# A chunked attention with a bilinear feed-forward: weights of tiles 2 and 3 by halves of rows, values in PSUM tiles of their own, and the Out product of block 1 by Strassen

## The chip, the cores and the metric

The kernel runs on one core of a Trainium2 chip, as one launch. The metric is the device time of that launch in microseconds (us). Engines are named as in the profile: PE is TensorE, with PEld its loading of weights; DVE is VectorE; ACT is ScalarE; POOL is GpSimd; SP is SyncE, whose queue issues nearly all the transfers.

## What is computed

Attention within chunks of 64 tokens for 8 batches, 8 heads, 576 tokens and a head size of 64; then a bilinear feed-forward over all 4608 tokens, with a model size of 512 and an inner size of 1536.

```python
q_c, k_c, v_c = (t.reshape(B, H, nc, 64, D) for t in (q, k, v))
scores = scale * np.matmul(q_c, k_c.transpose(0, 1, 2, 4, 3))
scores = scores - np.max(scores, axis=-1, keepdims=True)
attn = np.exp(scores)
attn = attn / (np.sum(attn, axis=-1, keepdims=True) + 1e-09)
x = np.matmul(attn, v_c)          # then (B, H, S, D) -> (B * S, H * D)
a = x @ w_a
b = x @ w_b
out = (a * b) @ w_out
```

Inputs and output are fp32. The kernel multiplies in bf16 and accumulates in fp32.

## The kernel before

**Tiling.** The 4608 tokens are nine blocks K of 512. A block is made by two attention units of 256 tokens each, so there are 18 units; unit u belongs to block u // 2. In the feed-forward the inner size is 12 tiles (ft) of 128 and the model size four tiles of rows (kt). The weights are kept in bf16 in six pairs: wa[i] and wb[i] serve tiles 2i and 2i + 1.

**One block of the feed-forward.** `ffn(K, ft)` (L415) takes two PSUM banks. `ffn_products` (L393) makes b and a, four matmuls of 512 columns each; `ffn_close` (L407) lets ACT copy b to SBUF and DVE multiply it by a, which gives ab[ft]. The four banks F are handed out in turn by `nextF` (L108), so a bank comes free when its reader of two tiles ago is done. The normalised attention of a block is in xT[K % 3]; a matmul of 512 columns reads both of its units.

**The Out product** comes in two forms. The plain one (`outs`, L441, and `out_products`, L420) takes 12 matmuls of 512 columns for each of four groups of 128 tokens. `outs_fast(K, t)` (L471) does Strassen's scheme on 2 x 2 blocks: seven products of six matmuls with 256 columns, for two groups of tokens at once, called for t = 0 and t = 1. It needs sums of the weights (`wsum`, by `sum_wo`, L453: four instructions for each of six pairs) and of ab (`asum`, by `sum_ab`, L463: three DVE instructions per pair of tiles). In it ACT copies the products m3 and m4 out, POOL adds them (w, L525), DVE adds the third product p1 to w (L526), and DVE and POOL make the four outputs. Blocks 0 and 1 are done in the plain form, blocks 2 to 8 by Strassen. `wsum` lies over slots 2 to 5 of the weights' staging ring `wst`, and `asum` over slots 6 to 9, where w_out's pairs 0 to 3 are staged: a sum of ab can be written only when the sums of those pairs have been read from there.

**Order.** The whole program is under a manual schedule: each engine executes its instructions in the order in which the code issues them. The stages that the change touches:

- The prologue (L551 to L638) does units 0 and 1 from the first block's heads, in quarters. `half_values` (L368) makes the values of heads 4 to 7 in one call, `half_normalise` (L383) divides them by the sums into xT[0], and `fill` (L536) keeps PE at work on zeros. Tiles 0 and 1 of block 0 start on row tiles 0 and 1 (L640 to L653) and go on with rows 2 and 3. `queue_w` (L569) issues the loads of weights on SP's queue and `land_w` (L573) casts them on POOL: pair 0 by halves of the rows, pair 1 by halves of the columns, the others whole.
- Block 0's Out product (L757 to L779) is run together with unit 2's attention.
- Block 1's feed-forward (L792 to L829) is done in two halves of 256 tokens for tiles 0 to 9, then whole for tiles 10 and 11. Between these loops POOL casts units 5, 6 and 7 (`cast_unit`) and makes sums of w_out (`some_sums`), and SP's queue gets transposes (`turn_unit`) and loads of later units (`load_unit`).
- Block 1's Out product is L836 to L840, with `slot(5, None)` behind its first group. A `slot` (L690) makes sums and values of one unit and the scores of the next; its normalisations and exponentials are put on a list, and `step()` (L709) issues one of them, before each tile.

Of the kernel before, what the change touches and what calls it, by code (L numbers as in the profile page):

```python
# [11 lines left out]
def kernel(  # L12
# [10 lines left out]
    nc = tc.nc  # L23
# [74 lines left out]
    asum = asum.rearrange("p (i n t) -> p i n t", i=NP, n=5)  # L98
    part = buf("part", [128, 2, 5, HF], FP32)

    state = {"f": 0, "b": 0, "o": 0, "w": 2}

    def ring(name, bufs):
        i = state[name]
# [260 lines left out]
        s = slice(mm * 256, mm * 256 + 256)  # L365
        nc.scalar.activation(out=inv[hu][:, :, s], in_=lns[:, :, s], func=AF.Exp, scale=-1.0)

    def half_values(hu):  # L368
        for mm in range(2):
            for g in range(4):  # L370
                c = mm * 256 + g * 64
                for cl in range(2):
                    for j in range(2):
                        h = 2 * mm + j
                        nc.tensor.matmul(
                            PA[j * 64:j * 64 + 64, cl, c:c + 64],
                            vb[hu][cl * 64:cl * 64 + 64, g * 256 + h * 64:g * 256 + h * 64 + 64],
                            E[hu][cl * 64:cl * 64 + 64, j, c:c + 64],
                            start=True,
                            stop=True,  # L380
                        )

    def half_normalise(hu, mm):  # L383
        s = slice(mm * 256, mm * 256 + 256)
        nc.vector.tensor_tensor(  # L385
            out=xT[0][:, 2 * hu + mm, :].rearrange("p (g c t) -> p c g t", g=4, c=2),
            in0=PA[:, :, s].rearrange("p c (g t) -> p c g t", g=4),
            in1=inv[hu][:, :, s].rearrange("p c (g t) -> p c g t", g=4),
            op=MULT,
        )  # L390
# [69 lines left out]
            c0, c1, op = ((1, 3, SUB), (2, 0, SUB), (0, 3, ADD))[part - 1]  # L460
            eng.tensor_tensor(out=y[:, part + 1], in0=b[:, c0], in1=b[:, c1], op=op)

    def sum_ab(i):  # L463

        a = ab2[i].rearrange("p f (h t) -> p (f h) t", h=2)
        y = asum[:, i]
        nc.vector.tensor_tensor(out=y[:, 4], in0=a[:, 0], in1=a[:, 3], op=ADD)
        nc.vector.tensor_tensor(out=y[:, 0:2], in0=a[:, 0:2], in1=a[:, 2:4], op=ADD)  # L468
        nc.vector.tensor_tensor(out=y[:, 2:4], in0=a[:, 1:3], in1=a[:, 0:4:3], op=SUB)  # L469

    def outs_fast(K, t):  # L471
        c = t * 128
        m3, m4, w, y1, y2 = [part[:, t, n, :] for n in range(5)]
        oa, ob = ring("o", osb), ring("o", osb)
        V, A, G = nc.vector, nc.scalar, nc.gpsimd

        def product(a, b, o=None, pairs=range(NP)):
            o = nextF()[:, 0:HF] if o is None else o
            for i in pairs:
                nc.tensor.matmul(  # L480
                    o, a(i)[:, c:c + 128], b(i), start=(i == 0), stop=(i == NP - 1)
                )
            return o

        def of_ab(f, h):
            return lambda i: ab2[i][:, f, h * HF:(h + 1) * HF]

        def of_wo(f, h):
            return lambda i: wo[i][:, f, h * HF:(h + 1) * HF]

        def of_asum(n):
            return lambda i: asum[:, i, n]

        def of_wsum(n):
            return lambda i: wsum[:, i, n]

        def add(eng, out, in0, in1, op=ADD):
            eng.tensor_tensor(out=out, in0=in0, in1=in1, op=op)  # L498

        if K == NBLK - 1 and t == 1:  # L500

            A.copy(out=m3, in_=product(of_ab(0, 0), of_wsum(2)))
            A.copy(out=m4, in_=product(of_ab(1, 1), of_wsum(3)))
            add(G, w, m3, m4)
            add(V, oa[:, HF:DM], product(of_asum(0), of_wo(1, 1)), m3)
            add(G, y1, w, oa[:, HF:DM], SUB)
            add(V, ob[:, 0:HF], product(of_asum(1), of_wo(0, 0)), m4)
            add(G, y2, w, ob[:, 0:HF], SUB)
            p1 = product(of_asum(4), of_wsum(4))
            store(K, 2 + t, ob, 0, HF)  # L510
# [12 lines left out]
        product(of_asum(4), of_wsum(4), p1, (NP - 1,))  # L523
        A.copy(out=m4, in_=p4)  # L524
# [26 lines left out]
    with tc.manual_schedule():  # L551
# [21 lines left out]
        def land_w(i, halves=1, xs=(0,)):  # L573

            c = 256 // halves
            for x in xs:
                for h in range(halves):
                    for n, w in (("b", wb), ("a", wa)):
                        kts, st = staged[n, i][x]
                        copy(  # L580
                            G,
                            w[i][:, kts[0]:kts[-1] + 1, h * c:h * c + c],
                            st[:, :, h * c:h * c + c],
                        )

        def queue_wo(i):
            staged["o", i] = load_wo(i, nc.sync)
# [40 lines left out]
        quad_scores(3)  # L628
        expo(1, 1)
        half_inverse(0, 1)  # L630
        half_values(0)
        for mm in range(2):
            half_normalise(0, mm)
# [6 lines left out]
        B0 = [(nextF(), nextF()) for _ in range(2)]  # L640
        spare = PS[:, 0, :]
        for of in "ba":
            for kt in range(2):
                for ft in range(2):
                    ffn_products(0, ft, (0, 1), (kt,), B0[ft], of)
        half_values(1)
        for mm in range(2):
            half_normalise(1, mm)
        fill(3, spare, 256)
        for ft in range(2):  # L650
            for kt in range(2, NKT):
                ffn_products(0, ft, (0, 1), (kt,), B0[ft])
            ffn_close(0, ft, (0, 1), B0[ft])  # L653
        queue_w(3)


# [55 lines left out]
                fn(*a)  # L712

        for ft in range(1, NFT):
            if ft > 1:
                ffn(0, ft)
            if ft in (1, 2, 3, 4, 5):
                land_w(ft, 2 if ft == 1 else 1)
# [39 lines left out]
        for f0 in range(0, NFT, 2):  # L758

            for tgs in ((0, 1), (2, 3)):  # L760
# [139 lines left out]
```

## Time and profile before

| | us |
|---|---|
| median of 13 runs (313.19 to 315.03) | 314.36 |
| the profiled execution | 314.5 |
| its span, first to last instruction | 312.6 |
| PE busy in the span | 301.6 |
| DVE busy | 186.9 |
| ACT busy | 135.1 |
| POOL busy | 123.7 |

The span is 1.9 us shorter than the execution's time. The mean granted clock of TensorE is 0.999 of full speed. The table counts busy time alone; which wait ends last in a stage is read from the timelines.

Where the stages lie, by PE's timeline: the feed-forward of block 0 begins at 12.9 us, its Out product at 37.3, block 1 at 50.0, block 1's Out product at 74.8, block 2 at 85.9. Blocks 3 to 7 then take about 31.9 us each.

In a line of a timeline stand the start, the time from the start of the first to the end of the last instruction of the group, the engine, the line of the kernel, the operation, the tile written and the tiles read, shapes and the count; in brackets the idle time of the engine just before, and what ended it. "SPq" is SP's queue of DMA issues. A line of code can be that of a helper: L170 is every copy or cast, L498 every add of `outs_fast`.

### The profile page before, as it was taken

The page shows a single profiled execution, that of the slowest core. Times are in us where ns is not written, and L with a number is a line of the kernel's source. Part 1 is how long each engine was busy: PE and PEld are TensorE (multiplying, and loading weights), DVE is VectorE, ACT ScalarE, POOL GpSimd, SP SyncE. Part 2 cuts the span into 40 slices and gives each one's busy share as a digit, 9 for nine tenths or more (in the row PEclk, how much of TensorE's full clock was granted, in tenths as well). Part 3 has the DMA queues.
Part 4 walks back from the last instruction along what each step waited for, and adds up shares of the span by engine and source line. Part 5 has one row for each costly group of instructions (what it writes and reads, how often), then busy time and mean ns, then how long its engine had stood idle before and what let it go on. Part 6 is the DMA issues. An engine that isn't in the chain of part 4 may idle for free.

```text
span 312.6 us, 7316 instructions
## 1 busy us (share of the span) xinstructions
PE 301.6 (96%) x2897; PEld 178.9 (57%) x2930; DVE 186.9 (60%) x373; ACT 135.1 (43%) x232; POOL 123.7 (40%) x151
## 2 busy tenths in 40 slices
PE   6889999999999999999999999999999999999995
PEld 3444457884444486448644764476446744674474
DVE  3544325544369655866596649664967476746663
ACT  3822245655246533562355326532644164313220
POOL 2667757966576128302720273017401400040023
PEclk9999999999999999999999999999999999999999
DMA  7999999999999999989898339933600410020003
GB/s 261 294 348 388 380 307 221 215 248 222 238 214 288 209 235 231 234 187 205 236 251 186 73 143 230 237 68 136 136 0 2 96 41 1 2 112 25 0 1 136
DMA packets 144819, 55.01 MB, mean 176 GB/s; under 512 B 126224, under 2 KB 138768, under 8 KB 144784
## 3 DMA queue, kind: packets, MB, share of 16 engines
q1 hardware_dynamic: 143696, 53.49, 68.5%
q10 hardware_dynamic: 1088, 1.05, 1.0%
q8 instruction: 23, 0.38, 0.5%
q14 instruction: 12, 0.10, 0.1%
HBM read 37.75 MB, written 9.44 MB: 151 GB/s over the span
## 4 chain that ended last, share of the span: by engine, by line
PE 88%; DMA 5%; SPq 2%; issue 1%; POOL 1%; ACTq 0%; ACT 0%; DVE 0%; POOLq 0%; DVEq 0%
PE F L399 57%; PE F L480 20%; PE F L421 7%; DMA f<-in_k_dram 3%; DMA wst<-in_moe_w_a_dram 2%; PE F L252 2%; PE PS L235 2%; PE PA L268 1%; SPq L155 1%; SPq L147 1%; POOL part L498 0%; POOL vb L170 0%; ACTq L140 0%; PE F L195 0%; SPq L217 0%
## 5 line engine op out<-in xcount | busy, mean ns | idle before, releaser
L399 PE MATMUL F<-xT,wa 128*128 128x512 bf16 (+1 forms) x470 | 112.5, 361 | 2.2 <-POOL wa L170 1.2
L399 PE MATMUL F<-xT,wb 128*128 128x512 bf16 (+1 forms) x444 | 110.8, 360 | 1.6 <-DVE xT L385 0.4
L410 ACT CAST bsb<-F 128x512 bf16<-128x512 f32 (+1 forms) x118 | 64.5, 548 | 104.9 <-PE F L399 104.6
L411 DVE TENSOR_TENSOR ab<-F,bsb 128x512 bf16<-128x512 f32 (+1 forms) x118 | 75.6, 643 | 52.8 <-PE F L399 44.7
L399 PEld LDWEIGHTS <-wa 128*128 128x128 bf16 x472 | 46.1, 98 | 49.8 <-POOL wa L170 1.9
L399 PEld LDWEIGHTS <-wb 128*128 128x128 bf16 x472 | 44.6, 98 | 43.4 <-issue 0.5
L498 POOL TENSOR_TENSOR part<-part 128x256 f32<-128x256 f32 x14 | 10.2, 725 | 128.7 <-ACT part L524 127.7
L170 POOL CAST qkb<-f 128x1024 bf16<-128x1024 f32 (+1 forms) x35 | 34.8, 1006 | 27.2 <-DMA f<-in_k_dram 13.8
L480 PEld LDWEIGHTS <-wst 128*128 128x128 bf16 x420 | 41.1, 98 | 4.9 <-issue 0.2
L480 PE MATMUL F<-wst 128*128 128x256 bf16 x252 | 33.5, 273 | 0.0
L287 DVE TENSOR_TENSOR xT<-PA,inv 128x512 bf16<-128x512 f32 x32 | 21.8, 683 | 19.4 <-ACT inv L282 19.4
L498 DVE TENSOR_TENSOR osb<-F,part 128x256 f32<-128x256 f32 x56 | 22.3, 419 | 11.0 <-POOL part L498 9.5
L498 POOL TENSOR_TENSOR part<-part,osb 128x256 f32<-128x256 f32 x28 | 19.8, 727 | 11.4 <-DVE osb L498 11.3
L170 POOL CAST vb<-f 128x1024 bf16<-128x1024 f32 (+2 forms) x22 | 20.0, 912 | 8.5 <-DMA f<-in_v_dram 7.1
L480 PE MATMUL F<-wst,ab 128*128 128x256 bf16 x168 | 22.8, 273 | 0.0
L469 DVE TENSOR_TENSOR wst<-ab 128x512 bf16<-128x512 bf16 x42 | 22.2, 530 | 0.0
L421 PE MATMUL F<-wo,ab 128*128 128x512 bf16 x93 | 21.1, 379 | 0.4 <-issue 0.3
L278 ACT ACTIVATE lns<-F 128x512 f32<-128x512 f32 x30 | 16.3, 594 | 10.7 <-PE F L252 10.7
L246 ACT ACTIVATE E<-PS 128x1024 bf16<-128x1024 f32 (+1 forms) x20 | 18.8, 942 | 4.5 <-PE PS L235 3.5
L480 PE MATMUL F<-wo,wst 128*128 128x256 bf16 x168 | 20.6, 273 | 0.0
L468 DVE TENSOR_TENSOR wst<-ab 128x512 bf16<-128x512 bf16 x42 | 20.5, 489 | 0.0
L498 DVE TENSOR_TENSOR part<-F,part 128x256 f32<-128x256 f32 x15 | 6.4, 425 | 21.5 <-POOL part L498 21.5
(62 smaller groups left out, 197.3 us busy)
## 6 DMA issues: line engine op xcount, KB each, us to landing
out_dram<-osb SPq DMA_DIRECT2D x31, 256.0 KB, 3.1
f<-in_q_dram SPq DMA_DIRECT2D x28, 256.0 KB, 4.2
f<-in_v_dram SPq DMA_DIRECT2D x28, 256.0 KB, 4.9
f<-in_k_dram SPq DMA_DIRECT2D x24, 256.0 KB, 4.3
wst<-in_moe_w_out_dram SPq DMA_DIRECT2D x6, 512.0 KB, 7.7
wst<-in_moe_w_b_dram SPq DMA_DIRECT2D x5, 512.0 KB, 7.8
wst<-in_moe_w_a_dram SPq DMA_DIRECT2D x5, 512.0 KB, 8.1
f<-in_v_dram SPq DMA_DIRECT2D x16, 128.0 KB, 3.9
```

The source lines that it names most:

```text
L170: eng.tensor_copy(out=out, in_=in_)
L246: nc.scalar.activation(out=e[:, :, s], in_=PS[:, :, s], func=AF.Exp, scale=scale)
L278: nc.scalar.activation(out=lns[:, cl, :], in_=SU[cl], func=AF.Ln)
L287: nc.vector.tensor_tensor(out=x.rearrange("p m (g c t) -> p c g m t", g=2, c=2)[:, cl], in0=PA[:, cl, :].rearrange(shape, g=2, m=4), in1=i ...
L399: nc.tensor.matmul(bank[:, 0:n], w[ft // 2][:, kt, (ft % 2) * 128:(ft % 2) * 128 + 128], x[:, kt, us[0] * 256:us[0] * 256 + n], start=(kt ...
L410: nc.scalar.copy(out=bT[:, 0:n], in_=banks[0][:, 0:n])
L411: nc.vector.tensor_tensor(out=ab[ft][:, us[0] * 256:us[0] * 256 + n], in0=banks[1][:, 0:n], in1=bT[:, 0:n], op=MULT)
L421: nc.tensor.matmul(o, ab[ft][:, tg * 128:(tg + 1) * 128], wo[ft // 2][:, ft % 2, :], start=(ft == 0), stop=(ft == NFT - 1),)
L468: nc.vector.tensor_tensor(out=y[:, 0:2], in0=a[:, 0:2], in1=a[:, 2:4], op=ADD)
L469: nc.vector.tensor_tensor(out=y[:, 2:4], in0=a[:, 1:3], in1=a[:, 0:4:3], op=SUB)
L480: nc.tensor.matmul(o, a(i)[:, c:c + 128], b(i), start=(i == 0), stop=(i == NP - 1))
L498: eng.tensor_tensor(out=out, in0=in0, in1=in1, op=op)
```

## The change

It has four parts.

1. **Weights.** Pair 1 (tiles 2, 3) is loaded and cast by halves of the rows, as pair 0 is. Tiles 2 and 3 are computed as a pair over the four banks: first rows 0 and 1 of both, then rows 2 and 3. The ring of staging slots starts at 0 instead of 2, so that w_out's pairs are staged where they were.
2. **Values in the prologue.** `half_values` takes the half mm and the tile it writes. For heads 4 to 7 the two halves go to PA and PS, each normalised right after; the three fills behind them are left out.
3. **Sums of w_out.** The eight of pairs 0 and 1 are made on DVE, beside block 0's Out product; POOL makes the other sixteen.
4. **Block 1's Out product by Strassen.** The first two instructions of `sum_ab` run during block 1's feed-forward, the third one for all six pairs in a row behind it; `slot(5, None)` comes between the two calls of `outs_fast`, and POOL's and SP's work around them is put in another order. In the last block's second call of `outs_fast` two DVE adds change places.

```diff
-    state = {"f": 0, "b": 0, "o": 0, "w": 2}
+    state = {"f": 0, "b": 0, "o": 0, "w": 0}
...
-    def half_values(hu):
-        for mm in range(2):
-            for g in range(4):
...
+    def half_values(hu, mm, o):
+
+        for g in range(4):
+            c = mm * 256 + g * 64
...
-    def sum_ab(i):
+    def sum_ab(i, parts=(4, 0, 2)):
...
+        for part in parts:
+            if part == 4:
+                V.tensor_tensor(out=y[:, 4], in0=a[:, 0], in1=a[:, 3], op=ADD)
+            elif part == 0:
+                V.tensor_tensor(out=y[:, 0:2], in0=a[:, 0:2], in1=a[:, 2:4], op=ADD)
+            else:
+                V.tensor_tensor(out=y[:, 2:4], in0=a[:, 1:3], in1=a[:, 0:4:3], op=SUB)
...
             add(V, y1, p1, y1)
-            add(V, y2, p1, y2)
             add(V, oa[:, 0:HF], product(of_asum(3), of_wsum(1)), y1)
             store(K, t, oa)
+            add(V, y2, p1, y2)
             add(V, ob[:, HF:DM], product(of_asum(2), of_wsum(0)), y2)
...
-        queue_w(1)
+        queue_w(1, range(2))
+        queue_w(1, range(2, NKT))
         queue_w(2)
...
-        land_w(0, 1, (1,))
+        land_w(0, (1,))
+        land_w(1, (0, 1))
...
-        half_values(1)
+        two = [(nextF(), nextF()) for _ in range(2)]
+        ffn_rows(two, 0, range(2), "ba")
+
+        o = [t[:, :, 0:256] for t in (PA, PS)]
         for mm in range(2):
-            half_normalise(1, mm)
-        fill(3, spare, 256)
...
+            half_values(1, mm, o[mm])
+            half_normalise(1, mm, o[mm])
+        ffn_rest(two, 0, range(2, NKT))
+        two = [(nextF(), nextF()) for _ in range(2)]
+        for i in range(2):
+            for m in "ba":
+                ffn_products(0, 2 + i, (0, 1), range(2), two[i], m)
+        ffn_rest(two, 2, range(2, NKT))
...
+        fast_sums, wo_sums = wo_sums[:8], wo_sums[8:]
...
                     evacuate_pairs(2, 1, t[1], (A, V))
+                    for a in fast_sums:
+                        sum_wo(*a, V)
...
             ffn(1, ft, (1,))
             if ft == 2:
                 slot(None, 4)
+            if ft % 2:
+                sum_ab(ft // 2, (4, 0))
         cast_unit(6, (0,))
-        some_sums(2)
+        some_sums(24)
         cast_unit(6, (1,))
-        some_sums(2)
         cast_unit(6, (2,))
         turn_unit(6)
         load_unit(7, (1, 2))
         load_unit(8, (0,))
-        cast_unit(7, (0, 1))
+        cast_unit(7, (0,))
         for ft in range(10, NFT):
             step()
             ffn(1, ft)
             if ft == 10:
                 slot(4, 5)
+        sum_ab(NP - 1, (4, 0))
+        step()
+        for i in range(NP):
+            sum_ab(i, (2,))
+        step()
+        outs_fast(1, 0)
+        cast_unit(7, (1,))
         turn_unit(7)
         load_unit(8, (1, 2))
         load_unit(9, (0,))
         cast_unit(7, (2,))
-        some_sums(24)
-        cast_unit(8, (0, 1))
-        for tg in range(4):
-            step()
-            outs(1, (tg,))
-            if tg == 0:
-                slot(5, None)
+        slot(5, None)
+        step()
+        outs_fast(1, 1)
         cast_unit(8)
```

`ffn_rows` and `ffn_rest` are new: the first makes the products of given rows for a pair of tiles, b of both before a of both; the second makes the remaining rows of each tile in turn and closes it.

More of the change, by code (lines that the diff above doesn't have):

```diff
@@ L366, in half_inverse, with half_normalise @@
         nc.scalar.activation(out=inv[hu][:, :, s], in_=lns[:, :, s], func=AF.Exp, scale=-1.0)
-    def half_values(hu):
-        for mm in range(2):
-            for g in range(4):
[L371 to L383, printed above, removed]
+    def half_values(hu, mm, o):
+        for g in range(4):
+            c = mm * 256 + g * 64
+            for cl in range(2):
+                for j in range(2):
+                    h = 2 * mm + j
+                    nc.tensor.matmul(
+                        o[j * 64:j * 64 + 64, cl, g * 64:g * 64 + 64],
+                        vb[hu][cl * 64:cl * 64 + 64, g * 256 + h * 64:g * 256 + h * 64 + 64],
+                        E[hu][cl * 64:cl * 64 + 64, j, c:c + 64],
+                        start=True,
+                        stop=True,
+                    )
+    def half_normalise(hu, mm, o):
         s = slice(mm * 256, mm * 256 + 256)
@@ L386, in half_normalise @@
             out=xT[0][:, 2 * hu + mm, :].rearrange("p (g c t) -> p c g t", g=4, c=2),
-            in0=PA[:, :, s].rearrange("p c (g t) -> p c g t", g=4),
+            in0=o.rearrange("p c (g t) -> p c g t", g=4),
             in1=inv[hu][:, :, s].rearrange("p c (g t) -> p c g t", g=4),
@@ L461, in sum_wo @@
             eng.tensor_tensor(out=y[:, part + 1], in0=b[:, c0], in1=b[:, c1], op=op)
-    def sum_ab(i):
+    def sum_ab(i, parts=(4, 0, 2)):
         a = ab2[i].rearrange("p f (h t) -> p (f h) t", h=2)
         y = asum[:, i]
-        nc.vector.tensor_tensor(out=y[:, 4], in0=a[:, 0], in1=a[:, 3], op=ADD)
-        nc.vector.tensor_tensor(out=y[:, 0:2], in0=a[:, 0:2], in1=a[:, 2:4], op=ADD)
-        nc.vector.tensor_tensor(out=y[:, 2:4], in0=a[:, 1:3], in1=a[:, 0:4:3], op=SUB)
+        V = nc.vector
+        for part in parts:
[5 more added lines that the diff above has]
+                V.tensor_tensor(out=y[:, 2:4], in0=a[:, 1:3], in1=a[:, 0:4:3], op=SUB)
     def outs_fast(K, t):
@@ L571, in queue_w, with land_w @@
                 staged.setdefault((n, i), []).append((kts, load_w(src, i, kts, nc.sync)))
-        def land_w(i, halves=1, xs=(0,)):
-            c = 256 // halves
+        def land_w(i, xs=(0,)):
             for x in xs:
[L577 to L584, printed above, removed]
+                for n, w in (("b", wb), ("a", wa)):
+                    kts, st = staged[n, i][x]
+                    copy(G, w[i][:, kts[0]:kts[-1] + 1, :], st)
         def queue_wo(i):
@@ L630 @@
         half_inverse(0, 1)
-        half_values(0)
+        o = [PA[:, :, mm * 256:mm * 256 + 256] for mm in range(2)]
         for mm in range(2):
-            half_normalise(0, mm)
+            half_values(0, mm, o[mm])
+        for mm in range(2):
+            half_normalise(0, mm, o[mm])
         fill(1, F[0], 256)
@@ L638, with ffn_rows, ffn_rest @@
             half_inverse(1, mm)
[L640 to L645, printed above, removed]
-        half_values(1)
-        for mm in range(2):
-            half_normalise(1, mm)
-        fill(3, spare, 256)
[L650 to L653, printed above, removed]
+        def ffn_rows(banks, f0, kts, of):
+            for m in of:
+                for kt in kts:
+                    for i in range(2):
+                        ffn_products(0, f0 + i, (0, 1), (kt,), banks[i], m)
+        def ffn_rest(banks, f0, kts):
+            for i in range(2):
+                for kt in kts:
+                    ffn_products(0, f0 + i, (0, 1), (kt,), banks[i])
+                ffn_close(0, f0 + i, (0, 1), banks[i])
+        two = [(nextF(), nextF()) for _ in range(2)]
+        ffn_rows(two, 0, range(2), "ba")
+        o = [t[:, :, 0:256] for t in (PA, PS)]
+        for mm in range(2):
+            half_values(1, mm, o[mm])
+            half_normalise(1, mm, o[mm])
+        ffn_rest(two, 0, range(2, NKT))
+        two = [(nextF(), nextF()) for _ in range(2)]
+        for i in range(2):
+            for m in "ba":
+                ffn_products(0, 2 + i, (0, 1), range(2), two[i], m)
+        ffn_rest(two, 2, range(2, NKT))
         queue_w(3)
@@ L714 @@
         for ft in range(1, NFT):
-            if ft > 1:
+            if ft > 3:
                 ffn(0, ft)
-            if ft in (1, 2, 3, 4, 5):
-                land_w(ft, 2 if ft == 1 else 1)
+            if ft in (2, 3, 4, 5):
+                land_w(ft)
             if ft in (1, 2):
```

## The prediction

> **What bounds the kernel now.** I read the page first, then the chain of waits, then the timelines of GpSimd (POOL), SyncE's queue (SP), VectorE (DVE) and TensorE (PE) around 75 to 95 us, where most of the change lies.
>
> ```profile
> PE 301.6 (96%) x2897; PEld 178.9 (57%) x2930; DVE 186.9 (60%) x373; ACT 135.1 (43%) x232; POOL 123.7 (40%) x151
> DMA  7999999999999999989898339933600410020003
> ```
>
> PE is busy nearly always, so only PE work taken out, or a new PE wait, changes the time. The DMA row matters as much: one digit is 7.8 us, and the engines are full until about 140 us. Until then a load lands when the stream reaches it, not when PE would like it.
>
> ```profile
> 74.97 2.59 PE F L421 x12
> 77.56 0.34 PE F L252 x4
> 77.90 0.28 PE PA L268 x31
> 78.18 0.16 issue
> 78.34 7.72 PE F L421 x35
> 110.29 9.17 PE F L480 x84
> ```
>
> These are pieces of the chain (start, length). Block 1's Out product by the plain form is 2.59 + 7.72 = 10.3 us; block 2's by Strassen is 84 matmuls in 9.17 us, 109 ns each. Hence the most that the new product can save on PE: 10.37 (48 x 216 ns) - 9.17 = 1.2 us.
>
> GpSimd's timeline in that stretch:
>
> ```profile
> 74.55 1.04 POOL L170 CAST qkb<-f 128x1024 bf16<-128x1024 f32 x1 [2.59 <-DMA f<-in_q_dram]
> 77.72 1.04 POOL L170 CAST qkb<-f 128x1024 bf16<-128x1024 f32 x1 [0.23 <-DMA f<-in_k_dram]
> 80.08 1.03 POOL L170 CAST vb<-f 128x1024 bf16<-128x1024 f32 x1
> 82.00 1.04 POOL L170 CAST qkb<-f 128x1024 bf16<-128x1024 f32 x1 [0.89 <-DMA f<-in_q_dram]
> 87.33 1.04 POOL L170 CAST qkb<-f 128x1024 bf16<-128x1024 f32 x1 [4.29 <-DMA f<-in_k_dram]
> 89.19 1.04 POOL L170 CAST vb<-f 128x1024 bf16<-128x1024 f32 x1 [0.81 <-PE F L399]
> ```
>
> The reader is to see the brackets: the casts of unit 6 (q, k, v) and unit 7 (q, k, v) stand in this order and wait for their loads. Unit 7's q cannot be cast before 82.0, its k before 87.3. The last bracket names a matmul, but the buffer's last reader is values(4) at 72.4 us, so I take this too for the load of v. Nobody waits for these casts now. SP's queue says why the loads are late:
>
> ```profile
> 76.73 1.69 SPq L124 DMA_DIRECT2D f<-in_q_dram  x2
> 78.79 2.91 SPq L217 DMA_TRANSPOSE qkT<-qkb  x1
> 81.74 1.21 SPq L124 DMA_DIRECT2D f<-in_k_dram  x2
> 83.00 3.25 SPq L124 DMA_DIRECT2D f<-in_v_dram  x2
> ```
>
> q of unit 7 is issued at 76.73, k and v behind unit 6's transpose. Last, one steady product by Strassen, on POOL and on DVE:
>
> ```profile
> 112.64 0.72 POOL L498 TENSOR_TENSOR part<-part 128x256 f32<-128x256 f32 x1 [3.11 <-ACT part L524]
> 114.23 1.41 POOL L498 TENSOR_TENSOR part<-part,osb 128x256 f32<-128x256 f32 x2 [0.87 <-DVE osb L498]
> ```
> ```profile
> 113.39 0.42 DVE L498 TENSOR_TENSOR part<-F,part 128x256 f32<-128x256 f32 x1 [1.31 <-POOL part L498]
> 115.67 0.42 DVE L498 TENSOR_TENSOR osb<-F,part 128x256 f32<-128x256 f32 x1 [0.26 <-POOL part L498]
> ```
>
> POOL's add w = m3 + m4 (L525) starts everything: DVE's w += p1 (L526) ends 1.17 us after it starts (113.81 - 112.64) and frees the bank that the seventh product needs; the last output add ends 3.45 us after it starts (116.09 - 112.64).
>
> **What the Trainium skill says.** "TensorE: Matmul & The Clock Gate", architectural detail: GpSimd's queue is strictly first in, first out; the timeline agrees, the 82.00 cast holding all behind it. The same page, Part 1: an array idle for a window of about 3.4 us falls to half clock; no run here shows it, the longest wait on PE being 1.5 us. "SBUF - State Buffer", Who interferes with whom: a VectorE instruction with two SBUF inputs and a GpSimd instruction that reads SBUF exclude each other. The trace agrees: at 90.88 us the sum L467 took 1.41 us beside a 1.26 us POOL sum, against 0.29 at 111.12.
>
> **The change part by part.**
>
> *Weights of tiles 2, 3.* PE idles 1.19 us before 20.91, waiting for the cast of wa[1]. By halves of rows, the pair can start on rows 0, 1. But a[1]'s rows 2, 3 are the last bytes of the same stream (landing about 20.2), cast by 20.85; seven 216 ns matmuls follow, so the pair ends near 22.4 instead of 23.5. Then wa[2]: the casts of later weights wait for DMA at 24.32, 25.68, 27.03, 1.36 us apart, so I put wa[2]'s landing at 22.95 and its cast's end at 24.0. PE wanted it at 24.4 before. Estimate: 1.1 us gained, 0.75 lost again, 0.35 stays; bounds 0.2 and 1.1. Two more DMA issues at some 0.5 us on SP lie under the backlog.
>
> *Values in tiles of their own, no fill.* The 1.4 us of fill end at 16.97; the next needs, xT rows 2, 3 and wa[0]'s cast (17.02), hold the second matmul anyway. At most 0.1 us.
>
> *Sums of wo 0, 1 on DVE.* Eight adds, estimated at 0.35 to 0.7 us each from DVE's fp32 rows, about 4 us (6 with exclusion) after 42.3 us, where DVE idles 4.8 us. POOL's remaining 16 are paced as before by the same casts, so transposes and loads keep their times. Nothing, bounds 0 to 0.5.
>
> *sum_ab in block 1's second half.* Two adds per two tiles, 0.55 us pipelined (0.29 and 0.42 rows); DVE is busy 5.57 of 14 us there. POOL is busy 8.6 of 14 and may stretch them: 0 to 1 us, unless covered by what follows.
>
> *The third sums, six in a row.* PE ends tile 11 at 74.97 - 0.35 = 74.6. DVE: ab[11] until 76.1, two sums, a normalise, then six at 0.34 us spacing: to 79.4. PE has 30 matmuls (3.3 us) before it needs the first; the sixth of asum(3) waits to 79.4, so asum(3) ends near 79.7, not 78.5: 1.2 to 1.3 us with nothing else in the way.
>
> *POOL's adds behind the casts: the main term.* Cast 7 q stays ahead of outs_fast(1, 0). Its w add is ready for at 77 to 78 but can start only at 83.0. Then DVE w to 84.2, and the seventh product, whose bank it frees (four banks in turn), 84.2 to 84.9; PE idles from 79.7 to 84.2. Slot 5 takes 0.62, the next m3 waits for asum(3)'s bank to 85.8. In outs_fast(1, 1) the w add stands behind casts 7 k and 7 v: 89.19 + 1.0 = 90.2. PE, done with six products at 89.75, resumes at 91.4 and ends at 92.1. SP's two new stores go ahead of transpose 7, but scores(7) comes over 8 us after block 2's start: covered.
>
> *normalise(5, 1)* now stands behind the last output add: 90.2 + 3.45 = 93.65, then one more normalise at 0.61 spacing: 94.3. Block 2's first matmul needs it. Before, it began at 85.89. So +8.4 us. This contains the 0.35 gained, the 1.2 saved, the 1.25 of the third sums: all end before the load that decides.
>
> *Block 2.* Block 2 took 33.4 us (86.05 to 119.46), block 3 31.9; 0.69 of it are PE waits for DVE at 94.67 and 97.89, after sums beside POOL's last five. Those five are gone: -0.7, bounds 0 and -1.1.
>
> *The tail.* oa is stored one DVE add (0.34) earlier, ob unchanged: -0.2, bounds 0 and -0.35.
>
> Sum: 8.4 - 0.7 - 0.2 = +7.5 on the profiled execution's 314.5 (span 312.6 and 1.9 around it): 322.0. The 13 runs' median, 314.36, is 0.14 below; I leave it at 322.0.
>
> **Rivals.**
> A: the same, and colder. PE's 4.5 us idle is near the page's window; at half clock the 30 matmuls before the second hold take 6.4 us instead of 3.3, and DVE exclusion adds. Worth 0.5 to 2.5: about 323.5. For: idle longer than any seen. Against: the granted clock is 1.00 in every stretch before, and the second hold covers much.
> B: the loads are in time, or partly. Without POOL's hold: -0.35 - 1.2 + 1.25 + 2.05 (PE's end to DVE's last add, 119.3 to 120.68, and normalise 0.61 with 0.05 wake) - 0.9 = +0.85: 315.3. With the first hold alone the second w add starts at 88.1, block 2 at 92.2: 319.9. Against: brackets of 0.89 and 4.29 us on DMA.
> C, not slower: the whole load stream stands earlier. It decides if unit 7's q lands before 77 us and its v before 83.3, weights too. Then -1.1 - 1.2 + 1.25 + 2.05 - 1.1 - 0.2 = -0.3: 314.2, or below it if the sums find DVE free. For: two casts move off POOL's way. Against: a full DMA row; nothing removes bytes.
>
> **How the numbers follow.** The forecast 0.60 (320.3 to 323.5), A 0.17, B 0.16, C 0.07. Range 317.5 to 324.5: it leaves out C, B's lower half and A's top. A measurement here tells 0.2%, 0.6 us. Slower: forecast, A and B, 0.93; C splits into 0.04 faster and 0.03 same.
>
> **What would show it.** In the changed trace: PE's wait near 20.9 nearly gone, and a new short one near 24; in block 1's product, a PE wait of 4 to 5 us before the last six matmuls of outs_fast(1, 0), with POOL's first L498-type add right behind a cast near 83; a second add near 90; block 2's first matmul near 94.3, waiting for a normalise. If POOL's w add starts before 80, the main step is wrong and B stands; if q of unit 7 lands before 77, C. A granted clock below 1.00 between 80 and 98 us would be A.

## The result, and the profile after

The changed kernel takes 321.98 us (median; single runs 320.9 to 325.4) against 314.51 of the kernel before in the same and later series. The ratio is 1.0241, with a 95% interval of 1.0218 to 1.0265: it is slower by 2.4%, or 7.5 us. The longest run, 325.38 us, counts as a slow one and is not in the ratio. The profiled execution took 322.32 us, with a span of 320.5, which is 7.9 more than the span before.

In the changed kernel's lines, L399 is still the feed-forward's matmul; the matmul of `outs_fast` is L485 (was L480), its adds L503 (was L498), the sums of w_out L458 and L461, the sums of ab L470, L472 and L474 (the third one). L411 is the product a * b, L287 the normalise, L529 ACT's copy of m4. The page of the changed kernel, rows of parts 1 and 2:

```profile
PE 303.6 (95%) x2927; PEld 181.9 (57%) x2960; DVE 201.4 (63%) x405; ACT 136.3 (43%) x236; POOL 122.6 (38%) x149
PEclk9999999999689999999999999999999999999999
DMA  7999999999999974988799817971700220011003
```

DVE has 14.5 us more work than before (201.4 - 186.9). The granted clock of TensorE, flat before, dips in slices 11 and 12, from 80 to 96 us. The page's PE busy time even rises: where the clock is halved, a matmul is counted for longer (eleven of `outs_fast` in 2.45 us at 87.62, in 1.36 at 76.98).

The chain of waits of the changed kernel, around block 1's Out product (start, length, what):

```profile
83.01 1.04 POOL qkb L170
84.06 0.69 POOL part L503
84.77 0.44 DVE part L503
85.25 1.44 PE F L485 x6
...
94.25 0.42 DVE osb L503
94.68 0.61 DVE xT L287
95.33 0.38 PE F L399
```

A cast on POOL, then POOL's add, then DVE's add, then PE's seventh product; and at the end DVE's last output add, the normalise, and block 2's first matmul. GpSimd's timeline of the same kernel shows what the cast waited for:

```profile
79.32 1.04 POOL L170 CAST qkb<-f 128x1024 bf16<-128x1024 f32 x1 [1.99 <-DMA f<-in_k_dram]
80.97 1.24 POOL L170 CAST vb<-f 128x1024 bf16<-128x1024 f32 x1 [0.62 <-DMA f<-in_v_dram]
83.01 1.04 POOL L170 CAST qkb<-f 128x1024 bf16<-128x1024 f32 x1 [0.80 <-DMA f<-in_q_dram]
84.02 0.72 POOL L503 TENSOR_TENSOR part<-part 128x256 f32<-128x256 f32 x1
87.44 1.04 POOL L170 CAST qkb<-f 128x1024 bf16<-128x1024 f32 x1 [0.43 <-DMA f<-in_k_dram]
89.76 1.04 POOL L170 CAST vb<-f 128x1024 bf16<-128x1024 f32 x1 [1.28 <-DMA f<-in_v_dram]
91.22 0.73 POOL L503 TENSOR_TENSOR part<-part 128x256 f32<-128x256 f32 x1 [0.41 <-ACT part L529]
```

TensorE's timeline of the same kernel has these waits (in brackets):

```profile
71.21 0.60 PE L399 MATMUL F<-xT,wa 128*128 128x256 bf16 x4 [0.67 <-DVE ab L411]
76.98 1.36 PE L485 MATMUL F<-wst,ab 128*128 128x256 bf16 x11
80.69 0.95 PE L485 MATMUL F<-wst 128*128 128x256 bf16 x3 [0.27 <-DVE wst L474]
82.54 1.06 PE L485 MATMUL F<-wst 128*128 128x256 bf16 x3 [0.89 <-DVE wst L474]
85.25 1.44 PE L485 MATMUL F<-wst 128*128 128x256 bf16 x6 [1.65 <-DVE part L503]
95.33 1.02 PE L399 MATMUL F<-xT,wb 128*128 128x512 bf16 x3 [1.87 <-DVE xT L287]
```

The second row is the start of block 1's Out product, 2.2 us later than the 74.80 of before: PE is late before it comes to the adds. Then it waits three times in the sixth and seventh product, and once more before block 2. And VectorE's timeline of the same kernel:

```profile
43.02 0.68 DVE L458 TENSOR_TENSOR wst<-wst 128x512 bf16<-128x512 f32 x1
45.47 1.52 DVE L458 TENSOR_TENSOR wst<-wst 128x512 bf16<-128x512 f32 x1
46.91 2.99 DVE L461 TENSOR_TENSOR wst<-wst 128x256 bf16<-128x256 f32 x3
49.82 1.28 DVE L287 TENSOR_TENSOR xT<-PA,inv 128x512 bf16<-128x512 f32 x2
79.46 3.69 DVE L474 TENSOR_TENSOR wst<-ab 128x512 bf16<-128x512 bf16 x6
```

The normalise that opens block 1 ran at 47.13 before; here it stands behind the sums of w_out until 49.82. The six third sums end at 83.15, 0.87 us before POOL's add begins. So two holds end nearly together. Which one costs the time can't be read from this profile alone, since a chain names only the last.

### The profile page after: what moved, and what is told of

The parts are those of the page before. It is cut to its first block, busy times and chain, and to the rows that moved or that the text cites. A ratio compares the mean times of both kernels' runs of the same rounds, so it can differ in the third digit from the quotient of the medians.

```text
span 320.5 us, 7428 instructions
## 1 busy us (share of the span) xinstructions
PE 303.6 (95%) x2927; PEld 181.9 (57%) x2960; DVE 201.4 (63%) x405; ACT 136.3 (43%) x236; POOL 122.6 (38%) x149
## 4 chain that ended last, share of the span: by engine, by line
PE 75%; DMA 12%; SPq 6%; DVE 3%; POOL 1%; issue 1%; ACTq 0%; ACT 0%; POOLq 0%; DVEq 0%
PE F L399 49%; PE F L485 22%; DMA wst<-in_moe_w_out_dram 5%; DMA wst<-in_moe_w_a_dram 3%; SPq L124 2%; DMA f<-in_k_dram 2%; DMA wst<-in_moe_w_b_dram 2%; PE F L252 2%; DVE wst L461 2%; SPq L217 1%; PE PS L235 1%; PE PA L268 1%; DMA f<-in_q_dram 1%; SPq L155 1%; SPq L147 1%
## 5 line engine op out<-in xcount | busy, mean ns | idle before, releaser
L399 PE MATMUL F<-xT,wb 128*128 128x512 bf16 (+1 forms) x443 | 111.3, 360 | 4.5 <-DVE xT L287 2.1
L399 PE MATMUL F<-xT,wa 128*128 128x512 bf16 (+1 forms) x470 | 113.5, 361 | 1.7 <-DVE ab L411 0.7
L411 DVE TENSOR_TENSOR ab<-F,bsb 128x512 bf16<-128x512 f32 (+1 forms) x118 | 75.5, 642 | 48.8 <-PE F L399 38.5
L399 PEld LDWEIGHTS <-wa 128*128 128x128 bf16 x472 | 46.0, 98 | 50.0 <-POOL wa L170 2.4
L399 PEld LDWEIGHTS <-wb 128*128 128x128 bf16 x472 | 44.5, 98 | 46.5 <-issue 2.5
L503 POOL TENSOR_TENSOR part<-part 128x256 f32<-128x256 f32 x16 | 11.6, 725 | 137.7 <-ACT part L529 136.7
L485 PEld LDWEIGHTS <-wst 128*128 128x128 bf16 x480 | 47.2, 98 | 10.1 <-DVE wst L474 2.6
L485 PE MATMUL F<-wst 128*128 128x256 bf16 x288 | 39.9, 276 | 3.0 <-DVE part L503 1.6
L503 DVE TENSOR_TENSOR osb<-F,part 128x256 f32<-128x256 f32 x64 | 25.6, 420 | 12.8 <-POOL part L503 10.5
L287 DVE TENSOR_TENSOR xT<-PA,inv 128x512 bf16<-128x512 f32 x32 | 21.8, 683 | 16.2 <-ACT inv L282 16.2
L503 POOL TENSOR_TENSOR part<-part,osb 128x256 f32<-128x256 f32 x32 | 22.6, 728 | 13.1 <-DVE osb L503 13.0
L485 PE MATMUL F<-wst,ab 128*128 128x256 bf16 x192 | 27.1, 281 | 0.0
L474 DVE TENSOR_TENSOR wst<-ab 128x512 bf16<-128x512 bf16 x48 | 24.6, 520 | 0.0
L472 DVE TENSOR_TENSOR wst<-ab 128x512 bf16<-128x512 bf16 x48 | 24.4, 509 | 0.0
L485 PE MATMUL F<-wo,wst 128*128 128x256 bf16 x192 | 23.6, 273 | 0.0
L503 DVE TENSOR_TENSOR part<-F,part 128x256 f32<-128x256 f32 x17 | 7.2, 424 | 24.5 <-POOL part L503 24.5
L485 PEld LDWEIGHTS <-ab 128*128 128x128 bf16 x192 | 19.2, 101 | 4.4
```

The costliest lines, as they stand in the source:

```text
L287: nc.vector.tensor_tensor(out=x.rearrange("p m (g c t) -> p c g m t", g=2, c=2)[:, cl], in0=PA[:, cl, :].rearrange(shape, g=2, m=4), in1=i ...
L399: nc.tensor.matmul(bank[:, 0:n], w[ft // 2][:, kt, (ft % 2) * 128:(ft % 2) * 128 + 128], x[:, kt, us[0] * 256:us[0] * 256 + n], start=(kt ...
L411: nc.vector.tensor_tensor(out=ab[ft][:, us[0] * 256:us[0] * 256 + n], in0=banks[1][:, 0:n], in1=bT[:, 0:n], op=MULT)
L472: V.tensor_tensor(out=y[:, 0:2], in0=a[:, 0:2], in1=a[:, 2:4], op=ADD)
L474: V.tensor_tensor(out=y[:, 2:4], in0=a[:, 1:3], in1=a[:, 0:4:3], op=SUB)
L485: nc.tensor.matmul(o, a(i)[:, c:c + 128], b(i), start=(i == 0), stop=(i == NP - 1))
```

## The experiments

Each kernel is compared with the kernel before, run beside it; the ratios carry 95% intervals. Loads land at different times from run to run (see the last section), so single profiles are read for their waits and the ratios for the time. Clock times of two profiles can't be set side by side as they stand: PE comes to block 1's Out product at 74.8 us in the kernel before, at 77.0 in the changed one and at 75.7 to 80.7 in its variants with Strassen's form. The stage from there to block 2's first matmul took 11.1 us before and 18.4 in the changed kernel (76.98 to 95.33). Where lines of code were added, the same work stands a few lines further on (L487 for L485, L505 for L503).

**POOL's adds of block 1 put on DVE.** This takes the adds out of the queue behind the casts.

```diff
         V, A, G = nc.vector, nc.scalar, nc.gpsimd
+        if K == 1:
+            G = V
```

> Changed kernel with POOL's three adds in each outs_fast of block 1 (w, y1, y2) put on DVE; nothing else. Theory (POOL's adds stand behind casts that wait for loads): the wait of 1.65 us before the seventh product and the second hold go, block 2 starts near 88.5 instead of 95.3, time 315 to 316.5. Rival 1 (the third sums in a row and the late normalise cost it): 321 to 322. Rival 2 (the halved clock costs it): between, as the idle time is shorter, 318 to 320.

Measured: 320.88 us, 1.0235 (1.0184 to 1.0287). The theory's 315 to 316.5 is missed, and the time is hardly better than the change's own 1.0241. The VectorE and TensorE timelines of this kernel:

```profile
81.29 2.92 DVE L474 TENSOR_TENSOR wst<-ab 128x512 bf16<-128x512 bf16 x6
84.14 0.41 DVE L505 TENSOR_TENSOR part<-part 128x256 f32<-128x256 f32 x1
86.23 1.14 DVE L505 TENSOR_TENSOR part<-part,osb 128x256 f32<-128x256 f32 x1
90.22 1.12 DVE L505 TENSOR_TENSOR part<-part 128x256 f32<-128x256 f32 x1 [0.58 <-ACT part L531]
```
```profile
83.26 1.29 PE L487 MATMUL F<-wst 128*128 128x256 bf16 x4 [0.88 <-DVE wst L474]
94.77 1.86 PE L399 MATMUL F<-xT,wb 128*128 128x512 bf16 x4 [2.03 <-DVE xT L287]
```

The wait for POOL is gone, and the row of third sums holds the add in its place: it begins at 84.14, right behind the row. That is no earlier than POOL's at 84.02, but PE came to the product at 78.72 here and at 76.98 there: counted from PE's coming, the add is 1.6 us sooner (5.42 us against 7.04). This profile is of the longest of the four runs, 323.45 us, so it shows where DVE stands in POOL's place and not how much the edit is worth. Two of the moved adds take 1.1 us instead of 0.42 beside POOL's casts, and the normalise still ends last. In this run block 2's first tile ran at half clock (four matmuls in 1.86 us, elsewhere 1.03).

**Both normalises of unit 5 before the second product.**

```diff
         slot(5, None)
-        step()
+        drain()
         outs_fast(1, 1)
```

> Changed kernel with both normalises of unit 5 issued before outs_fast(1, 1) instead of one before and one behind it. Theory: the 1.87 us that PE waits for that normalise at 95.3 go, since the last products end at 93.3 either way: 320.0, that is 1.7 to 2.0 less than the changed kernel. Rival (loads alone set block 2's start): no change, 321.5 to 322.5.

Measured: 317.70 us, 1.0129 (1.0075 to 1.0182). The ratio is 1.1 points, some 3.5 us, below that of the change, where 1.7 to 2.0 had been expected. PE goes from the last product straight to block 2, without a bracket (TensorE, then GpSimd of this kernel):

```profile
89.22 1.47 PE L485 MATMUL F<-wst 128*128 128x256 bf16 x12
90.53 1.03 PE L399 MATMUL F<-xT,wb 128*128 128x512 bf16 x4
```
```profile
79.14 1.04 POOL L170 CAST qkb<-f 128x1024 bf16<-128x1024 f32 x1 [1.12 <-DMA f<-in_q_dram]
81.35 0.97 POOL L503 TENSOR_TENSOR part<-part 128x256 f32<-128x256 f32 x1 [1.17 <-ACT part L529]
```

The wait itself was 1.87 us. What the rest is, if it is more than noise, stays open: by the two intervals the gain is 1.1 points give or take 0.6, which is 1.7 to 5.4 us and reaches down to what was expected. Two things besides the edit differ in this profile. The clock stayed at 1.00. And POOL had no hold here: PE came late, at 78.84, unit 7's q was cast at 79.14, and POOL's first add waited for ACT's copy and not for a load. This load is issued ahead of the edit, so its landing is not the edit's doing.

**The third sums in the loop** instead of six in a row.

```diff
             if ft % 2:
-                sum_ab(ft // 2, (4, 0))
+                sum_ab(ft // 2)
...
-        sum_ab(NP - 1, (4, 0))
+        sum_ab(NP - 1)
         step()
-        for i in range(NP):
-            sum_ab(i, (2,))
```

> Changed kernel with the third sums of ab made in the loop with the other two instead of six in a row behind it. Theory (POOL's add decides at 84.0 and 91.2): PE's two waits for the sums (0.27 and 0.89 us) become a longer wait for POOL's add, time unchanged within 0.5. Rival (the row of sums is on the path): 1.2 to 2 us less, 320.

Measured: 322.67 us, 1.0257 (1.0208 to 1.0305): no gain, as the theory had it, but not for its reason alone. TensorE and VectorE of this kernel:

```profile
71.86 0.60 PE L399 MATMUL F<-xT,wa 128*128 128x256 bf16 x4 [1.43 <-DVE ab L411]
79.86 1.02 PE L399 MATMUL F<-xT,wa 128*128 128x512 bf16 x4 [0.84 <-DVE ab L411]
```
```profile
77.06 0.95 DVE L472 TENSOR_TENSOR wst<-ab 128x512 bf16<-128x512 bf16 x1
77.94 1.27 DVE L474 TENSOR_TENSOR wst<-ab 128x512 bf16<-128x512 bf16 x1
79.13 0.68 DVE L411 TENSOR_TENSOR ab<-F,bsb 128x512 bf16<-128x512 f32 x1
```

The sums, stretched to 0.95 and 1.27 us beside a sum of w_out and a cast on POOL, now hold the product a * b behind them, whose bank PE needs. The cost moved into the loop; it was not removed.

**Unit 7's casts behind the two products.** POOL keeps its adds, DVE's work is untouched.

```diff
-        cast_unit(7, (0,))
         for ft in range(10, NFT):
...
         outs_fast(1, 0)
+        cast_unit(7, (0,))
+        slot(5, None)
+        step()
+        outs_fast(1, 1)
         cast_unit(7, (1,))
         turn_unit(7)
         load_unit(8, (1, 2))
         load_unit(9, (0,))
         cast_unit(7, (2,))
-        slot(5, None)
-        step()
-        outs_fast(1, 1)
```

> Changed kernel with the cast of unit 7's q behind outs_fast(1, 0) and those of its k and v, transpose 7 and the loads after it behind outs_fast(1, 1). POOL's first add then waits only for unit 6's v, cast by about 82.2, the second for nothing. Theory: block 2 starts near 91.3, 4 us sooner: 318. Rival (the sums, the normalise or the clock): 321 to 322.

Measured: 319.36 us, 1.0157 (1.0108 to 1.0207), 2.6 us less than the change; 4 were expected. POOL's hold is thus a cause, and not the whole. The profile is of the longest of the four runs (320.95 us). VectorE, GpSimd and TensorE of it:

```profile
78.57 4.31 DVE L474 TENSOR_TENSOR wst<-ab 128x512 bf16<-128x512 bf16 x6
81.71 0.89 POOL L503 TENSOR_TENSOR part<-part 128x256 f32<-128x256 f32 x1
85.64 2.53 PE L485 MATMUL F<-wst,ab 128*128 128x256 bf16 x11
89.83 0.73 POOL L503 TENSOR_TENSOR part<-part 128x256 f32<-128x256 f32 x1 [3.82 <-ACT part L529]
```

POOL's first add ran at 81.71, and the row of sums went on until 82.88: DVE had become the last. The second add waited for no cast any more but 3.82 us for ACT's copy, behind matmuls of PE at half clock: it came 4.19 us after the first matmul of its product, against 2.53 at full clock in the run with the early normalises (85.92 to 88.45). By these two figures the half clock cost an estimated 1.7 us here. The two of the four runs with a mean clock of 0.998 and 1.0 took 318.1 and 318.4 us, which is the theory's 318; the two at 0.987 and 0.995 took 321.0 and 320.3.

**Both of these edits together.**

> Changed kernel with unit 7's casts behind the two outs_fast (as in the run that did this alone, 319.4) and both normalises of unit 5 before outs_fast(1, 1) (alone 317.7); POOL keeps its adds. If the two costs add up: 315 to 316.5. If what remains is DVE's (the sums of ab, excluded by POOL's casts, and PE's late arrival): 317 to 318.

Measured: 316.31 us, 1.0066 (1.0039 to 1.0093). From 1.0241, the two edits took 0.8 and 1.1 points each, and 1.75 together: they nearly add up. The stage from the first product to block 2 took 12.6 us in this profile, against 18.4. What is left, 0.66%, is still slower than before. PE's waits in this profile were 1.5 us for the third sums and 0.8 for a * b.

**DVE's adds and the early normalises together.**

> Changed kernel with POOL's adds of block 1 on DVE and both normalises of unit 5 before outs_fast(1, 1). If POOL's hold and the late normalise are two causes in parallel, both out of the way give more than either alone (320.9, 317.7): 316 to 317, and the granted clock stays at 1.00. If the normalise was all of it, 317.7 as without DVE's adds.

Measured: 319.29 us, 1.0123 (1.0061 to 1.0186), the same as the normalises alone (1.0129). The two do not add up. PE's waits in this profile are for DVE (1.5 us for a * b, 1.4 for the add of p1, 0.8 for the third sums), whose queue got six more adds; that this made up for what POOL's hold gave back is argued, not shown. The clock fell to half between about 87 and 90.5 us here, so this part of the expectation failed too.

**The same without block 1's sums of ab.** This takes away DVE's share by itself.

```diff
             if ft % 2:
-                sum_ab(ft // 2, (4, 0))
...
         def of_asum(n):
+            if K == 1:
+                return of_ab(n % 2, 0)
             return lambda i: asum[:, i, n]
```

> Changed kernel with POOL's adds of block 1 on DVE, both normalises of unit 5 early, and without block 1's sums of ab: its Strassen products read ab itself in their place, so the 18 DVE sums of block 1 are left out and block 1's output is not the reference's. Against the run with the first two edits alone (319.3). Theory now (DVE's sums pace block 1's second half and its Out product): 315 to 316, PE's waits for ab and wst before 90 us gone, and the first product of block 1's Out starts by 77.5. Rival (loads, or PE's own work): 318.5 to 319.5.

Measured: 314.24 us, 0.9987 (0.996 to 1.0013). Against the ratio with the sums, 1.0123, they cost 1.4 points, or 4.3 us, give or take 2 by the two intervals. TensorE of this kernel:

```profile
75.92 2.13 PE L487 MATMUL F<-wst,ab 128*128 128x256 bf16 x18
86.53 1.03 PE L399 MATMUL F<-xT,wb 128*128 128x512 bf16 x3
```

From the first product to block 2 it is 10.6 us with no wait for `wst` or `ab`, against 11.1 in the kernel before (74.80 to 85.89): 0.5 saved, not 1.2, and slot 5 between the two halves took 1.3 us (80.50 to 81.77) where it had taken 0.8 (77.56 to 78.34). The wait for the normalise ahead of block 1, 1.1 us in this profile, takes more than that. So even with its sums for nothing, block 1's product by Strassen only draws level with the kernel before.

**The sums of w_out on DVE alone**, in the kernel before (the third part of the change; the edit is the one of the diff).

> Kernel before with the third part alone: the eight sums of w_out's pairs 0 and 1 on DVE beside block 0's Out product. Theory: block 1's first matmul waits 0.3 to 2 us for normalise(2, .) behind them; block 2's 0.7 us of waits go: 314.5 to 316. Rival (hidden, as DVE idles there): 313.6 to 314.

Measured: 315.25 us, 1.0021 (1.0001 to 1.0041): a loss of 0.2%, by an interval that just leaves out 1. PE waited 1.1 us for normalise(2, 0 and 1) before block 1, and had no wait for DVE in block 2.

**The changed kernel without its fourth part**: block 1's Out product plain, the order of POOL's and SP's work as before. Of the fourth part, only the two adds that changed places in the last block stay so.

> Changed kernel with its fourth part undone: block 1's Out product in the plain form, POOL's and SP's work around it in the old order; the first three parts stay (POOL has eight sums of w_out fewer). Theory (most of the loss is in part 4, a smaller share in part 3): 314.5 to 316, since DVE's eight sums hold the normalise before block 1 by 0.3 to 2 us and block 2 loses its 0.7 us of waits. Rival (parts 1 to 3 are free or a gain): 313.5 to 314.2.

Measured: 315.15 us, 1.0004 (0.998 to 1.0028). Parts 1 to 3 together can't be told from no change; the loss lies in part 4.

**The sums of w_out moved into block 1's first half**, with DVE's adds and the early normalises.

```diff
             ffn(1, ft, (0,))
+            if ft > 1:
+                sum_wo(*fast_sums[ft - 2], V)
```

> The same with the eight sums of w_out on DVE moved from block 0's Out product into block 1's first half, one behind each of tiles 2 to 9. Theory: PE's wait for normalise(2, .) before block 1 goes, and PE comes to block 1's Out product 1 to 2 us sooner: 314.5 to 316, 1 to 2 less than without the move. Rival (the time is made up by loads or by exclusion with POOL elsewhere): no change, 316 to 317.

Measured: 319.46 us, 1.0133 (1.0072 to 1.0193): no gain over 1.0123. The wait before block 1 was gone, but PE waited for a * b four times, 2.5 us in all: DVE has no room there either while POOL casts.

**PE kept busy in its idle time.**

```diff
+        if (K, t) == (1, 0):
+            fill(4, PS[:, 0, :], 256)
         add(V, oa[:, 0:HF], product(of_asum(3), of_wsum(1)), y1)
         store(K, t, oa)
+        if (K, t) == (1, 0):
+            fill(6, PS[:, 0, :], 256)
```

> Changed kernel with ten matmuls on zeros in PE's idle time in outs_fast(1, 0): four before the sixth product, six before the seventh, some 2.4 us. If PE's idle time is what halves the clock from 83.5 to 89.4 us, the clock stays at 1.00 there and the second w add starts 0.4 us sooner: 321 to 322. If the clock falls for another reason it falls all the same; if the idle time is too short for the ten, 323.

Measured: 322.59 us, 1.0251 (1.0212 to 1.029): no gain. But in the profiled run the clock stayed at 1.00. The windows of the changed kernel (stretch, then busy us of PE, PEld, DVE, ACT and POOL with counts, then the granted clock, DMA share and GB/s), against those of this one, and last those of the run with both edits together, which has no fills:

```profile
82.00:83.00 1.00, 0.41 (x2) 0.19 (x2) 1.00 (x3) 0.00 (x0) 0.21 (x1) 1.00 1.26 242
83.00:84.00 1.00, 0.55 (x2) 0.13 (x2) 0.15 (x1) 0.00 (x0) 0.99 (x1) 0.52 1.28 291
84.00:85.00 1.00, 0.00 (x0) 0.00 (x0) 0.23 (x1) 0.00 (x0) 0.74 (x2) 0.50 0.65 146
89.00:90.00 1.00, 1.00 (x7) 0.73 (x6) 0.49 (x1) 0.74 (x2) 0.24 (x1) 0.57 1.16 262
```
```profile
84.00:86.00 2.00, 2.00 (x11) 1.65 (x11) 1.09 (x3) 0.00 (x0) 1.13 (x3) 1.00 1.02 232
88.00:90.00 2.00, 2.00 (x21) 1.78 (x20) 0.60 (x1) 1.87 (x4) 0.83 (x1) 1.00 1.11 253
```
```profile
80.00:82.00 2.00, 0.92 (x6) 0.29 (x3) 2.00 (x3) 0.00 (x0) 2.00 (x2) 1.00 1.10 189
82.00:84.00 2.00, 1.46 (x12) 0.83 (x16) 1.71 (x5) 0.00 (x0) 0.64 (x2) 1.00 0.96 213
```

This run does not settle what the clock costs. That the fills kept the clock up is not shown: in the last profile it stayed at 1.00 without any, with PE busy for no more than 0.92 of the two microseconds from 80 to 82. The other three runs with fills had a mean clock of 0.994 and took 322.2 to 324.4 us; the profiled one, at 1.00, took 321.28. And the ten fills took 4.6 us of PE (1.89 and 2.75), not 2.4: the seventh product came at 85.99, 0.7 us later than in the change (85.25), though POOL's add ran at 84.02 in both profiles.

The single runs say more. In each of the seven variants with Strassen's form and its sums that have both kinds of runs, every run with a mean clock of 0.997 or more was shorter than every run below that, by some 1 to 2.5 us between the middles of the two groups: 316.1 to 316.9 against 317.8 and 318.5 us with both edits together, 320.2 against 322.6 to 322.8 with the third sums in the loop. In the plain form and without the sums the two kinds overlap. All runs of the change itself lie below, at 0.982 to 0.995. Whether the clock costs this time, or late loads lengthen both the waits and the time, these figures can't tell apart.

**The kernel before with one line moved.** The profile of before had shown that its last five sums on POOL stretch DVE's sums in block 2, and that POOL waits 4.3 us just before.

```diff
+        some_sums(24)
         cast_unit(7, (0, 1))
...
         cast_unit(7, (2,))
-        some_sums(24)
```

> Kernel before with one line moved: POOL's last five sums of w_out stand before the casts of unit 7 instead of behind them, where POOL waits 4.3 us for a load. Theory: block 2's two waits of PE for DVE (0.37 and 0.32 us), which come from DVE's sums beside these five, go: 313.7 to 314, 0.2% less than before. Rival (other exclusion takes their place, or the later cast of q delays a transpose): 314.3 to 315.

Measured: 313.73 us, 0.9977 (0.9962 to 0.9991): faster than both kernels, by 0.2% over the one before, with an interval that leaves out 1. VectorE of this kernel at the place where L467 had taken 1.41 us:

```profile
91.06 0.29 DVE L467 TENSOR_TENSOR wst<-ab 128x256 bf16<-128x256 bf16 x1
91.27 0.42 DVE L468 TENSOR_TENSOR wst<-ab 128x512 bf16<-128x512 bf16 x1
```

PE has no wait for DVE left in block 2.

## Why the prediction was right, and where it was not

The number, 322.0, was met. Its chain of steps is in the trace in its order, each about 1 us later than written: POOL's first add at 84.02 (83.0), its second at 91.22 (90.2), block 2 at 95.33 (94.3). For the first add this is the load stream, which ran later in this execution: unit 7's q was cast at 83.01 instead of 82.00. For the second it is 0.6 us of load (v's cast at 89.76 instead of 89.19) and 0.4 of the clock: the cast ended at 90.80, and the add waited on until 91.22 for ACT's copy of a product that PE made at half clock.

That the number was met so nearly is luck. Of the 7.9 us by which the span grew, block 2's start brought 9.4, where 8.4 had been forecast; block 2 gave back 1.0 instead of 0.7, the tail 0.4 instead of 0.2, and blocks 3 to 7, which the sum leaves out, 0.2. The range, and the path that the prediction named, are what its working supports.

- **Weights of tiles 2, 3.** PE's wait fell from 1.19 us to 0.21, with a new one of 0.28 at 24.40, as foreseen. From the first feed-forward matmul to block 0's Out product it took 24.15 us against 24.39: 0.24 gained, where 0.35 was written. This is one profile of each kernel and not shown as a gain: in the other profiles the waits for casts of weights came to between nothing and 1.9 us with this part, and to nothing and 0.9 without it, as the loads landed.
- **Values in tiles of their own, "at most 0.1".** As written: the second matmul behind them started 4.21 us after the first one of the feed-forward, 4.24 before. PE now waits 0.74 us for the normalise where it had the fills.
- **Sums of w_out on DVE, "nothing, bounds 0 to 0.5".** This step failed. The eight took 6.9 us (43.02 to 49.90), where 4 had been put and 6 with exclusion, and held the normalise in every profile that had them ahead of it: block 1 waited 0.26 us in the change's own, 1.1 in most others and 2.1 in one. In the run with this part alone the gain in block 2 hid most of it.
- **sum_ab in block 1's second half, "0 to 1 us", and "the sixth of asum(3) waits to 79.4".** The first held: PE lost 0.67 us to a * b. The second was sized without exclusion: the row took 3.69 us instead of 2.1 and ended at 83.15. Section "Who interferes with whom" of the Trainium skill's "SBUF — State Buffer" says that a DVE instruction with two SBUF inputs contends with a GpSimd instruction that reads SBUF, and this profile agrees: the six sums took 0.6 us each beside two casts (79.32 and 80.97), where single ones take 0.42. The price had not been put into this term. PE also came to the product at 76.98 and not at 74.6, so the one wait of 4 to 5 us that was to be the sign came as three, 2.8 us in all. Together these sums are worth 4.3 us, give or take 2, once the rest is out of the way.
- **POOL's adds behind the casts, "the main term".** The order was right, and moving the casts returns 2.6 us. But as the sole cause it fell: without POOL's adds 320.9 remained, not the 315.3 that rival B gave for it. DVE stood just behind POOL with a hold that ended 0.87 us earlier, so taking POOL's first add out of the way uncovers DVE's row. The prediction came out because the time goes by the later of two holds, and it had the later one right.
- **normalise(5, 1) late.** Written into the step as 0.61 us behind the last add. It was right in place and in size: from the second add's start to block 2 it took 4.11 us (91.22 to 95.33), where 4.06 had been put. PE's wait was 1.87 us. Moving the normalises returned some 3.5 us, give or take 2; whether it is worth more than the wait is not shown.
- **Block 2, -0.7.** 32.40 us (95.33 to 127.73, first matmul to first matmul) against 33.41 (85.89 to 119.30): -1.01, near the lower bound of -1.1. One moved line in the kernel before shows the cause by itself.
- **The tail, -0.2.** From the start of block 8 to the end, 33.05 us against 33.41: -0.36, at the far end of what was given.
- **Rival A.** Its sign, a clock below 1.00 between 80 and 98 us, came: half clock from 83 to 89.9 in the profile, and a mean below 1 in every run of the change. The forecast had put the clock at nothing. In the profile it delayed the second add by 0.4 us, as said above; in the run with the casts moved, an estimated 1.7. What it costs over all runs of the change stays open. The time is nearer to the forecast than to this rival's 323.5.
- **A reading.** The DMA row is called full until about 140 us; its digits are 7 to 9 up to the 22nd slice, 172 us. No term of the sum rests on it.

## What to carry to other kernels

A cheaper form of a product is paid for in other engines' queues: here at most 1.2 us of PE time were bought with 18 sums on DVE, beside POOL's casts, which exclude them, and with POOL's adds behind casts that wait for loads. When a wait ends, ask what ends just behind it: two holds within 1 us of each other can make a single undoing look like no cause (1.0235 with POOL's adds on DVE, 1.0257 with the row of sums broken up, against 1.0241), and undoing both, or taking one engine's work out altogether, shows more of their sizes. What needs no change of the algorithm may be had first: five POOL sums moved into a gap gave the 0.2% that the larger change did not.

## What the runs showed of the hardware

- The granted clock fell without one long idle time. In the microseconds from 80 to 83 PE was busy for 0.70, 0.57 and 0.41 of each, and then the clock was 0.50 until about 89.9, over 4 us after PE's work went on at 85.25. The Trainium skill, "TensorE: Matmul & The Clock Gate", Part 1, names an idle window of about 3.4 us as the condition; here partly busy microseconds were enough. They were not always: in the profile with both edits together PE was busy for 0.63, 0.28 and 0.51 of the microseconds from 80 to 83, and the clock stayed at 1.00. What decides it no run here shows.
- Exclusion of DVE and POOL also meets fp32 sums: a 128x512 sum of w_out took 0.68 us at 43.02 on DVE, and 1.52 at 45.47 beside a cast of 1.16 us.
- Loads landed at different times in runs of kernels with the same transfers ahead of them: unit 7's q could be cast at 79.14 us in one profile and at 84.15 in another.
